# Attention's products with V in plain fp32, two heads on two column halves, in a fused attention, Fourier and MLP kernel

## The chip, the core and the metric

The kernel runs on one core of a Trainium2 chip. The core has TensorE (PE in the rows, its weight loads as PEld), VectorE (DVE), ScalarE (ACT), GpSimd (POOL) and SyncE (SP, which issues DMAs here). The metric is the device time of one execution in microseconds, as the median of several runs. One further execution was taken by the profiler, and all rows come from it.

## The reference

Three blocks in a row: attention that keeps only scores close to the row's maximum, a Fourier mixing with an MLP, and a token mixing. The change lies in the first.

```python
def _attn_ref(q, k, v, tau):           # q, k, v: 4 x 8 heads x 576 x 64
    scores = 1.0 / np.sqrt(64) * np.matmul(q, k.transpose(0, 1, 3, 2))
    thresh = np.max(scores, axis=-1, keepdims=True) - tau
    scores = np.where(scores >= thresh, scores, -1000000000.0)
    attn = np.exp(scores - np.max(scores, axis=-1, keepdims=True))
    attn = attn / (np.sum(attn, axis=-1, keepdims=True) + 1e-09)
    return np.matmul(attn, v)

def _moe_ref(x, w_ch1, w_ch2):
    u = x + np.real(np.fft.fft(np.fft.fft(x, axis=1), axis=2))
    un = (u - mean(u)) / np.sqrt(var(u) + 1e-06)
    return u + np.maximum(un @ w_ch1, 0.0) @ w_ch2

def _moe2_ref(x, w_theta, w_tok_r, w_tok_i, w_ch):
    theta = x @ w_theta
    u = x + w_tok_r @ (x * cos(theta)) + w_tok_i @ (x * sin(theta))
    return u + np.maximum(u @ w_ch, 0.0)
```

## The kernel before

The 32 heads are taken as 16 pairs. A pair has nine score tiles of 128 queries by 576 keys. For each tile, TensorE makes the scores (lines 457 and 458: a high and a low part of the keys, in the type fp32r), VectorE takes the row maximum (467), ScalarE the exponential (472), VectorE the mask and the row sum (481), TensorE transposes the tile P in four blocks of 128 keys (488), and ScalarE copies the transposed block out of PSUM (499). The last 64 keys of each head are transposed apart (`rest_ops`, line 546) into `pt5`.

The products with V work on split numbers. `hi` writes the high part of the transposed P, rounded to fp32r, and `lo` subtracts it to get the low part (508; on VectorE, or for two tiles of nine on GpSimd from an extra copy `plain`, 503). V is split in the same way by ScalarE (416) and GpSimd (419), and high and low parts lie side by side as 128 weight columns. A pair has four products `pv`: for each head a half of 256 queries and a half of 320. Three of them (592, 595) multiply the 128 columns of V with the high and with the low part of P. The fourth, of head 0 and the first half (`WHOLE`), multiplies P as one fp32 number (583) for the four whole key blocks, and takes parts for the rest (587). A product comes out of PSUM in two pieces: ScalarE copies one 64-row part (601), VectorE adds the other (605). GpSimd multiplies the finished pair with the reciprocal row sums R (676) into `xT`.

When four pairs are done, a batch is done, and its Fourier transform (lines 723 to 946, tiles X, Y, u) runs among the work of later pairs; the last batch's runs after the last pair. Then come the MLP (h at line 1187, acc at 1207 to 1209) and the token mixing. The MLP's weights are widened on ScalarE, VectorE and GpSimd (1056 to 1090), from the end of the attention on.

The order on every engine is made before the program is written: `Plan.schedule` takes the operations with estimated costs, due times (`pr`) and a table of corrections `SHIFT`, lets an engine wait up to `PATIENCE` for an operation that is due earlier, and writes each engine's instructions in the order found. On the chip every engine keeps that order. Score tiles use two PSUM buffers, transposes and products share four banks (tag `O`).

Of the kernel before, what the change touches and what calls it, by code (L numbers as in the profile page):

```python
# [97 lines left out]
class Plan:  # L98
# [160 lines left out]
    PATIENCE = {"PE": 20, "DVE": 0, "ACT": 80, "POOL": 520, "SP": 460}  # L259


def attention_and_fft(pl, tc, ident, tb, pss, left, middle, right, qk, vv, cfk, cst, csr, u_d):
# [22 lines left out]
    Q, V, VR, xTs = {}, {}, {}, {}  # L285
# [120 lines left out]
    def load_v(p):  # L406
        loc = {}
        prio = [pr(9 * p - 9 + d if p else -8 + i, s) for i, (d, s) in enumerate(LOADS[7:])]

        def dma(e):  # L410
            VR[p] = loc["vr"] = new("vr", [128, 12, 64], f"vr{p}")
            e.dma_start(loc["vr"][:], vv[p])

        def hi(e):
            V[p] = new("v", [128, 12, 2, 64], f"v{p}", F32R)
            e.copy(V[p][:, :, 0], loc["vr"][:])

        def lo(e):
            e.tensor_sub(V[p][:, :, 1], loc["vr"][:], f32(V[p][:, :, 0]))

        pl.op(("vr", p), "SP", 1000, prio[0], dma, new=[("vr", p)], delay=8000)
        pl.op(("hv", p), "ACT", act(768, False), prio[1], hi, [("vr", p)], [("v", p)], [("vr", p)])
        pl.op(("lv", p), "POOL", pool(768), prio[2], lo, [("hv", p)], (), [("vr", p), ("v", p)])


    def pair(p):
        g0 = 9 * p
        st = {}

        def ptiles(h, half):  # L430
            return [(f"p{t}{h}{half}", p) for t in ("h" if (h, half) in WHOLE[p] else "hl")]

        def tile_ops(idx):
# [10 lines left out]
            parted = [d for d in dests if d[:2] not in WHOLE[p]]  # L444
# [46 lines left out]
            def hi(e):  # L491
                for h, half in fresh:
                    for t, _ in ptiles(h, half):
                        st[t[1], h, half] = new(t, [128, 4, 320 if half else 256], f"{t}_{p}",
                                                F32 if (h, half) in WHOLE[p] else F32R)
                    if not half:
                        st["r", h] = new("pt5", [128, 2, 320], f"pt5{p}_{h}", F32R)
                for h, half, qc, c0, w in dests:
                    e.copy(st["h", h, half][:, :, qc:qc + w], loc["T"][:, :, c0:c0 + w])

            def plain(e):
                tf = new("tf", [128, 4, 128], f"tf{p}_{idx}")
                e.copy(tf[:], loc["T"])
                loc["T"] = tf

            def lo(e):
# [7 lines left out]
            made = [x for f in fresh for x in ptiles(*f)] + [("pt5", p, h) for h, half in fresh if not half]  # L514
            hs = [x for d in dests for x in ptiles(*d[:2])]
# [10 lines left out]
            after, lo_on, src = "turn", "DVE", T  # L526
            if idx in YSET[p] and parted:
                src, after, lo_on = ("tf", k), "plain", "POOL"
                pl.op(("plain", k), "ACT", act(512), pr(g + 2, 5), plain, [("turn", k)], [src], [T])
            pl.op(("hi", k), "ACT", act(512, after == "turn") + 40 * (len(dests) - 1), pr(g + 2, 5), hi,  # L530
                  [(after, k)] + [("hi", (p, i)) for i in his], made, [src] + [x for x in hs if x not in made])
            if parted:
                w = 4 * sum(d[4] for d in parted)
                pl.op(("lo", k), lo_on, (dve if lo_on == "DVE" else pool)(w) + 40 * (len(parted) - 1), pr(g + 2, 8), lo,
                      [("hi", k)], (), [src] + hs)

        def rest_ops(h, idxs, g):
# [11 lines left out]
            def parts():  # L549
                if tail:  # L550
                    return [(st["r", i], slice(256, 320), loc["T"][:, 64 * i:64 * i + 64]) for i in range(2)]
                return [(st["r", h], slice(0, 256), loc["T"][:, 0:256])]

            def hi(e):
                for pt5, c, src in parts():
                    e.copy(pt5[:, 0, c], src)

            def lo(e):
                for pt5, c, src in parts():
                    e.tensor_sub(pt5[:, 1, c], src, f32(pt5[:, 0, c]))  # L560
# [7 lines left out]
            pl.op(("hi", k), "ACT", act(64) * 2 if tail else act(256), pr(g, 5), hi, [("turn", k)] + before, (), [T] + hs)  # L568
            pl.op(("lo", k), "DVE", dve(64) * 2 if tail else dve(256), pr(g, 8), lo, [("hi", k)], (), [T] + hs)

        def pv_ops(h, half, g):
# [26 lines left out]
            def copy(e):  # L598
                if (h, half) == (0, 0):
                    st["t"] = new("t", [128, S], f"t{p}")  # L600
# [1240 lines left out]
```

## Time and profile before

| what | value |
|---|---|
| median of 3 runs | 1022.69 us (1021.73 to 1023.72) |
| the profiled execution: time | 1019.57 us |
| its span, first to last instruction | 1017.7 us |
| mean granted clock of TensorE | 0.994 |
| TensorE busy | 979.6 us, 96% |
| VectorE busy | 702.4 us, 69% |
| ScalarE busy | 500.0 us, 49% |
| GpSimd busy | 293.9 us, 29% |

The profile page gives busy times over the whole span, then the costliest groups of instructions by line. A group names what is written and read (`O<-ph,v`), the shape, the count, the busy time and the mean of one instruction, and the idle time just ahead of it. Queries of the trace give busy times in chosen windows, instructions in order of time, and the chain of work that ended last. Durations of neighbours overlap, since engines are pipelined: what an instruction costs in a row of its like is the distance to the next start. The ends of matmuls are modelled.

### The profile page before, as it was taken

How to read it: one execution, taken by the hardware profiler on the slowest of the kernel's cores; microseconds unless marked ns; L12 is line 12 of the kernel's file. 1: busy time of each engine (PE TensorE's matmuls, PEld its weight loads, DVE VectorE, ACT ScalarE, POOL GpSimd, SP SyncE). 2: the span in 40 equal slices, each digit the busy share in tenths (PEclk: the TensorE clock that was granted, in tenths of full speed). 3: DMA queues.
4: the chain of work that ended last, by engine and by line, in shares of the span. 5: the costliest groups of instructions: out<-in, count | busy, mean ns of one | idle time of the engine just before them, and what ended most of it. 6: DMA issues, size and time to landing. Idle time of an engine off the chain costs nothing.

```text
span 1017.7 us, 16444 instructions
## 1 busy us (share of the span) xinstructions
PE 979.6 (96%) x5952; PEld 882.8 (87%) x5952; DVE 702.4 (69%) x1418; ACT 500.0 (49%) x961; POOL 293.9 (29%) x435
## 2 busy tenths in 40 slices
PE   5998899999999979999999999999999999999998
PEld 4888899999999868888888888899988999999998
DVE  6999999999999999997564452311245567766732
ACT  6898988889887744433231131111133333353410
POOL 5676867745864541012000000000000011121100
PEclk9999999999999989999999999999999999999999
DMA  7796555564652455454751353200305402011011
GB/s 204 211 226 150 151 132 149 148 182 116 159 130 58 129 185 174 166 185 167 244 201 61 102 193 113 73 1 1 119 19 209 164 22 61 29 43 56 17 41 48
DMA packets 49984, 123.15 MB, mean 121 GB/s; under 512 B 7088, under 2 KB 11760, under 8 KB 49520
## 3 DMA queue, kind: packets, MB, share of 16 engines
q1 hardware_dynamic: 49184, 119.08, 39.3%
q0 software_dynamic: 720, 3.02, 1.1%
q8 instruction: 47, 0.77, 0.3%
q14 instruction: 33, 0.27, 0.1%
HBM read 69.84 MB, written 23.66 MB: 92 GB/s over the span
## 4 chain that ended last, share of the span: by engine, by line
PE 74%; DVE 13%; ACT 6%; issue 2%; DMA 2%; POOL 1%; SPq 1%; ACTq 0%; DVEq 0%; POOLq 0%
PE h L1187 20%; PE y L1462 11%; PE acc L1209 7%; PE acc L1208 7%; PE acc L1207 7%; PE f L1526 5%; PE th L1338 5%; DVE c L467 4%; DVE P L481 4%; ACT P L472 2%; PE T L488 2%; PE ps L457 2%; PE ps L458 1%; PE O L592 1%; DVE pl L508 1%
## 5 line engine op out<-in xcount | busy, mean ns | idle before, releaser
L1187 PE MATMUL h<-uh,w 128*128 128x512 f32 (+1 forms) x640 | 199.1, 372 | 0.0
L1196 DVE SCALAR_TENSOR_TENSOR hl<-h,hh 128x512 fp32r<-128x512 f32 (+1 forms) x80 | 50.9, 637 | 156.5 <-ACT hh L1192 156.4
L1192 ACT ACTIVATE hh<-h 128x512 fp32r<-128x512 f32 (+1 forms) x80 | 44.4, 555 | 224.4 <-PE h L1187 224.4
L1187 PEld LDWEIGHTS h<-uh,w 128*128 128x128 f32 x640 | 118.9, 188 | 17.0
L457 PE MATMUL ps<-H,L 128*128 128x288 f32 x320 | 100.7, 332 | 20.5 <-DVE P L481 9.8
L1187 PE MATMUL h<-ul,w 128*128 128x512 f32 (+1 forms) x320 | 118.4, 370 | 0.0
L481 DVE SCALAR_TENSOR_TENSOR P<-ps,c,P 128x576 f32<-128x576 f32 x144 | 114.3, 809 | 5.1 <-ACT P L472 2.7
L472 ACT ACTIVATE P<-ps,c 128x576 f32<-128x576 f32 x144 | 106.3, 749 | 15.5 <-DVE c L467 14.7
L1207 PE MATMUL acc<-w,hh 128*128 128x512 f32 x288 | 113.6, 395 | 0.0
L1209 PE MATMUL acc<-w,hl 128*128 128x512 f32 x288 | 113.3, 393 | 0.0
L1208 PE MATMUL acc<-w,hh 128*128 128x512 f32 x288 | 113.2, 393 | 0.0
L467 DVE TENSOR_REDUCE c<-ps 128x1 f32<-128x576 f32 x144 | 106.5, 751 | 5.7 <-PE ps L458 4.6
L1462 PE MATMUL y<-w,z 128*128 128x288 f32 x768 | 109.8, 296 | 0.0
L1462 PEld LDWEIGHTS y<-w,z 128*128 128x128 f32 x768 | 104.5, 188 | 0.8
L458 PE MATMUL ps<-X,L 128*128 128x288 f32 x320 | 90.5, 300 | 0.3 <-DVE X L393 0.3
L488 PE MATMUL T<-ident,P 128*128 128x128 f32 x576 | 86.0, 278 | 2.2 <-DVE P L481 1.1
L457 PEld LDWEIGHTS ps<-H,L 128*128 128x128 f32 x320 | 61.9, 193 | 27.8 <-ACT H L390 7.2
L1370 POOL TENSOR_TENSOR tok<-tok 128x512 f32<-128x512 f32 x8 | 10.3, 1293 | 231.8 <-DVE tok L1342 122.2
L488 PEld LDWEIGHTS T<-ident,P 128*128 128x128 f32 x576 | 68.6, 142 | 6.6 <-DVE P L481 1.4
L1139 POOL TENSOR_SCALAR mv<-mv 128x1 f32<-128x1 f32 x18 | 9.3, 519 | 206.9 <-DVE mv L1135 206.6
L1187 PEld LDWEIGHTS h<-ul,w 128*128 128x128 f32 x320 | 60.2, 188 | 9.0
L1209 PEld LDWEIGHTS acc<-w,hl 128*128 128x128 f32 x288 | 54.0, 188 | 12.5 <-DVE hl L1196 0.2
(384 smaller groups left out, 2144.3 us busy)
## 6 DMA issues: line engine op xcount, KB each, us to landing
H<-hs SPq DMA_DIRECT2D x60, 160.0 KB
X<-raw SPq DMA_DIRECT2D x60, 160.0 KB
raw<-in_qk SPq DMA_DIRECT2D x15, 608.0 KB
vr<-in_vv SPq DMA_DIRECT2D x16, 384.0 KB
w<-w_d SPq DMA_DIRECT2D x6, 992.0 KB
mu<-u_d SPq DMA_DIRECT2D x18, 256.0 KB
ru<-u_d SPq DMA_DIRECT2D x18, 256.0 KB
x_d<-ru SPq DMA_DIRECT2D x18, 256.0 KB
```

Source lines behind the costliest of these rows:

```text
L457: e.matmul(ps[:, half, :HS], L[:, qo:qo + 128], H[:, ko:ko + HS], start=(j == 0), stop=False)
L458: e.matmul(ps[:, half, :HS], L[:, qo:qo + 128], X[:, ko:ko + HS], start=False, stop=(j == n - 1))
L467: e.tensor_reduce(loc["c4"][:, 0:1], loc["ps"][:, :, :HS], axis=AXES.XY, op=ALU.max, negate=True)
L472: e.activation(halves(), loc["ps"][:, :, :HS], AF.Exp, bias=loc["c4"][:, 0:1], scale=1.0)
L481: e.scalar_tensor_tensor(halves(), loc["ps"][:, :, :HS], loc["c4"][:, 1:2], halves(), op0=ALU.is_ge, op1=ALU.mult, accum_out=st["sums"][:, ...
L488: e.transpose(T[:, kt * 128:(kt + 1) * 128], P[:, kt * 128:(kt + 1) * 128], ident[:])
L1187: e.matmul(loc["ps"][:, :n], a, x[:, c, :n], start=(k == 0), stop=(k == 11))
L1196: e.scalar_tensor_tensor(loc["hl"][:, :n], loc["ps"][:, :n], 0.0, f32(loc["hh"][:, :n]), op0=ALU.max, op1=ALU.subtract)
L1207: e.matmul(a, hh[:, q], wh, start=(f == 0), stop=False)
L1208: e.matmul(a, hh[:, q], wl, start=False, stop=False)
L1209: e.matmul(a, hl[:, q], wh, start=False, stop=(f == NF - 1))
L1462: e.matmul(loc["ps"][:, half, :HS], z[:, cs], w, start=(n == 0 and m == 0), stop=(n == 8 and m == 2))
```

## The change

V and the transposed P are no longer split. One copy per tile writes the transposed P in plain fp32, and `plain`, both `lo` operations, the split of V, and the buffers for low parts are gone. The buffers for the transposed P are doubled. A pair has two products instead of four: one for the 256 queries of the first half and one for the 320 of the second, each over both heads. In each, five key blocks are multiplied in plain fp32 with 64 columns of V; head 0 writes partitions 0 to 63 of the bank and head 1 partitions 64 to 127, in turn. The result is multiplied with R by VectorE straight out of PSUM into `xT`; the copies, additions and the multiplication on GpSimd are gone. `PATIENCE` changes, and `SHIFT` gets further rows.

```diff
-    PATIENCE = {"PE": 20, "DVE": 0, "ACT": 80, "POOL": 520, "SP": 460}
+    PATIENCE = {"PE": 40, "DVE": 0, "ACT": 300, "POOL": 300, "SP": 210}
...
-    for t, n in dict(raw=2, hs=2, L=2, H=2, X=2, vr=2, v=2, P=3, pt5=2, t=1, R=1, tf=1,
+    for t, n in dict(raw=2, hs=2, L=2, H=2, X=2, vr=2, P=3, pt5=4, R=1,
...
-        for t in "h" if all((h, half) in WHOLE[p] for p in range(NP)) else "hl":
-            pl.tag(f"p{t}{h}{half}", 1)
+        pl.tag(f"p{h}{half}", 2)
...
-        pl.op(("hv", p), "ACT", act(768, False), prio[1], hi, [("vr", p)], [("v", p)], [("vr", p)])
-        pl.op(("lv", p), "POOL", pool(768), prio[2], lo, [("hv", p)], (), [("vr", p), ("v", p)])
...
-            def lo(e):
-                for h, half, qc, c0, w in parted:
-                    e.tensor_sub(st["l", h, half][:, :, qc:qc + w], loc["T"][:, :, c0:c0 + w],
-                                 f32(st["h", h, half][:, :, qc:qc + w]))
...
-        def pv_ops(h, half, g):
+        def pv_ops(half, g):
...
-                if whole:
-                    for kt in range(4):
-                        e.matmul(O[:, :n], VR[p][:, h * 6 + kt:h * 6 + kt + 2].rearrange("p a b->p (a b)"), st["h", h, half][:, kt],
-                                 start=(kt == 0), stop=False)
...
-                else:
-                    for kt in range(4):
-                        vk = v[:, h * 6 + kt].rearrange("p a b->p (a b)")
-                        for t in "hl":
-                            e.matmul(O[:, :n], vk, st[t, h, half][:, kt], start=(kt == 0 and t == "h"), stop=False)
...
+                O = loc["O"] = pl.bank([128, 512], f"O{p}_{half}")
+                for kt in range(5):
+                    for h in range(2):
+                        w, x = VR[p][:, h * 6 + (kt if kt < 4 else 4 + half)], st[h, half][:, kt] if kt < 4 else st["r", h][:, :n]
+                        e.matmul(O[64 * h:64 * h + 64, :n], w, x, start=(kt == 0), stop=(kt == 4))
+
+            def mul(e):
+                if (j, half) == (0, 0):
+                    xTs[b] = new("xT", [128, 4, S], f"xT{b}")
+                e.tensor_mul(xTs[b][:, j, a:a + n], loc["O"][:, :n], st["R"][:, a:a + n])
...
+            idxs = ((0, 2, 5, 7), (1, 3, 4, 6, 8))[half]
+            deps = [("hi", (p, i)) for i in idxs] + [("hi", (p, "r", i)) for i in ((0, 1), (0, 1, 2))[half]]
+            pl.op(("pv", k), "PE", 5 * TWO_PASS * n / 256 + 250, pr(g, 3), mms, deps + [("vr", p)], [O],
...
-        for h, gs in ((0, (g0 + 7, g0 + 8)), (1, (g0 + 11, g0 + 13))):
-            for half in range(2):
-                pv_ops(h, half, gs[half])
-        scale_op(g0 + 14)
+        for half in range(2):
+            pv_ops(half, g0 + 12 + 1.5 * half)
```

The names in the rows below: `ps` are scores, `P` masked tiles, `T` transposes, `O` products, `ph`, `pl` and `pt` (before) or `pt` alone (after) the transposed P, `pt5` its last key block, `v` the split V, `vr` V as loaded, `R` the reciprocal sums, `c` maxima. The number behind a name is the pair.

TensorE at the end of the last pair, before: the first two products follow the last scores.

```order
L458 MATMUL ps15_6_5296<-X15_4729,L15_4689 128x288
L583 MATMUL O15_0_0_5319<-ph00_15_5133,vr15_4605 128x256 x4
L587 MATMUL O15_0_0_5319<-pt515_0_5134,v15_4898 128x256 x3
L592 MATMUL O15_0_1_5333<-ph01_15_5135,v15_4898 128x320
L592 MATMUL O15_0_1_5333<-pl01_15_5136,v15_4898 128x320
L592 MATMUL O15_0_1_5333<-ph01_15_5135,v15_4898 128x320
L592 MATMUL O15_0_1_5333<-pl01_15_5136,v15_4898 128x320
L592 MATMUL O15_0_1_5333<-ph01_15_5135,v15_4898 128x320
L592 MATMUL O15_0_1_5333<-pl01_15_5136,v15_4898 128x320
L592 MATMUL O15_0_1_5333<-ph01_15_5135,v15_4898 128x320
L592 MATMUL O15_0_1_5333<-pl01_15_5136,v15_4898 128x320
L595 MATMUL O15_0_1_5333<-pt515_0_5134,v15_4898 128x320 x2
```

The same place after, behind all transposes of the pair:

```order
L580 MATMUL R15_0_4640<-ident_66,R15_4619 128x128 x4
L540 MATMUL O15_0_4650<-pt15_00_4385,vr15_4248 64x256
L540 MATMUL O15_0_4650<-pt15_10_4423,vr15_4248 64x256
L540 MATMUL O15_0_4650<-pt15_00_4385,vr15_4248 64x256
L540 MATMUL O15_0_4650<-pt15_10_4423,vr15_4248 64x256
L540 MATMUL O15_0_4650<-pt15_00_4385,vr15_4248 64x256
L540 MATMUL O15_0_4650<-pt15_10_4423,vr15_4248 64x256
L540 MATMUL O15_0_4650<-pt15_00_4385,vr15_4248 64x256
L540 MATMUL O15_0_4650<-pt15_10_4423,vr15_4248 64x256
L540 MATMUL O15_0_4650<-pt515_0_4386,vr15_4248 64x256
L540 MATMUL O15_0_4650<-pt515_1_4424,vr15_4248 64x256
L582 MATMUL R15_1_4670<-ident_66,rr15_4601 128x128
```

The products moved behind the transposes of the whole pair, and the heads stand in turn.

VectorE among the first tiles of pair 8, before, with the additions (605) and low parts (508, 560) of pairs 7 and 8:

```order
L605 TENSOR_TENSOR t7_2551<-O7_1_0_2669,t7_2551 64x256
L467 TENSOR_REDUCE c48_3_2732<-ps8_3_2719 128x1
L508 TENSOR_TENSOR pl11_7_2524<-T7_8_2652,ph11_7_2523 128x4x128
L467 TENSOR_REDUCE c48_4_2755<-ps8_4_2736 128x1
L869 TENSOR_TENSOR u0_0_1_2772<-xt0_0_1_2727,sm0_0_2657 128x256
L871 TENSOR_TENSOR u0_0_1_2772<-xt0_0_1_2727,dm0_0_2255 128x4x63
L873 TENSOR_TENSOR u0_0_1_2772<-xt0_0_1_2727,dm0_0_2255 128x4
L481 SCALAR_TENSOR_TENSOR P8_2_2681,sums8_2575<-ps8_3_2719,c48_3_2732,P8_2_2681 128x576
L481 SCALAR_TENSOR_TENSOR P8_4_2777,sums8_2575<-ps8_4_2736,c48_4_2755,P8_4_2777 128x576
L605 TENSOR_TENSOR t7_2551<-O7_1_1_2759,t7_2551 64x320
L560 TENSOR_TENSOR pt58_0_2713<-T58_0_2804,pt58_0_2713 128x256
L467 TENSOR_REDUCE c48_5_2832<-ps8_5_2814 128x1
```

The same place after:

```order
L451 TENSOR_REDUCE c48_1_2383<-ps8_1_2367 128x1
L460 TENSOR_SCALAR c48_1_2383<-c48_1_2383,tb_71 128x1
L451 TENSOR_REDUCE c48_4_2398<-ps8_4_2374 128x1
L465 SCALAR_TENSOR_TENSOR P8_0_2265,sums8_2229<-ps8_1_2367,c48_1_2383,P8_0_2265 128x576
L465 SCALAR_TENSOR_TENSOR P8_4_2402,sums8_2229<-ps8_4_2374,c48_4_2398,P8_4_2402 128x576
L545 TENSOR_TENSOR xT1_1514<-O7_0_2387,R7_2319 128x256
L545 TENSOR_TENSOR xT1_1514<-O7_1_2346,R7_2319 128x320
L451 TENSOR_REDUCE c48_5_2423<-ps8_5_2411 128x1
```

Between maxima and masks only the two multiplications of pair 7 are left, behind the masks of pair 8's first five tiles.

## Rows read from the trace of the kernel before

**Rows 1.** The page's part 1: busy us (share of the span) xinstructions

```profile
PE 979.6 (96%) x5952; PEld 882.8 (87%) x5952; DVE 702.4 (69%) x1418; ACT 500.0 (49%) x961; POOL 293.9 (29%) x435
```

**Rows 2.** Busy us by window; at the end clock, DMA share, GB/s

```profile
core 0: us, PE busy (x) PEld busy (x) DVE busy (x) ACT busy (x) POOL busy (x), PEclk, DMA share, GB/s
...
45.00:100.00 55.00, 49.52 (x349) 44.99 (x348) 51.54 (x120) 49.60 (x104) 41.07 (x65) 1.00 0.78 195
100.00:200.00 100.00, 95.14 (x707) 89.44 (x706) 96.33 (x229) 88.86 (x187) 72.59 (x114) 1.00 0.54 141
200.00:300.00 100.00, 97.88 (x738) 93.23 (x738) 96.18 (x232) 86.80 (x182) 67.63 (x105) 1.00 0.59 152
...
345.00:390.00 45.00, 38.21 (x247) 33.21 (x246) 42.32 (x84) 21.02 (x39) 18.72 (x20) 0.92 0.61 198
390.00:1018.00 628.00, 623.46 (x3406) 552.28 (x3404) 337.31 (x576) 184.97 (x316) 45.75 (x48) 1.00 0.30 99
```

**Rows 3.** Line L583, plain fp32 products: ns min/median/max, first and last start

```profile
L583 PE MATMUL O<-ph,vr x128: 377/379/484, 24.1 to 343.6; 128*128 128x256 f32 x128
```

**Rows 4.** Chain of waits, 40 to 130 us: start us, us, what

```profile
55.83 7.79 DMA X<-raw
...
122.11 1.73 PE O L583 x8
```

**Rows 5.** TensorE in order of time, last pair: start us, us, what

```profile
341.98 1.99 PE L583 MATMUL O<-ph,vr 128*128 128x256 f32 x8 [0.21 <-DVE pt L560]
...
344.17 0.31 PE L592 MATMUL O<-ph,v 128*128 128x320 f32 x1
...
345.63 1.03 PE L488 MATMUL T<-ident,P 128*128 128x128 f32 x8
...
350.47 0.28 PE L592 MATMUL O<-ph,v 128*128 128x256 f32 x1
...
351.66 0.31 PE L592 MATMUL O<-ph,v 128*128 128x320 f32 x1
...
353.13 0.40 PE L849 MATMUL Yt<-xho,cts 128*128 128x258 f32 x2
```

**Rows 6.** TensorE in order of time, 336.2 to 336.6 us

```profile
336.28 0.28 PE L821 MATMUL Xo<-ctr,eys 128*31 128x258 f32 x1
336.40 0.28 PE L821 MATMUL Xo<-ctr,exs 128*31 128x258 f32 x1
336.53 0.27 PE L546 MATMUL T<-ident,P 128*128 128x128 f32 x1
```

**Rows 7.** Groups of instructions: busy us, mean ns | idle before us

```profile
L508 DVE TENSOR_TENSOR pl<-T,ph 128x512 fp32r<-128x512 f32 (+1 forms) x96 | 55.4, 594 | 0.3
...
L508 POOL TENSOR_TENSOR pl<-tf,ph 128x512 fp32r<-128x512 f32 x32 | 41.2, 1288 | 11.2 <-ACT ph L499 7.3 <-PE T L488 2.4 <-issue 1.3
...
L419 POOL TENSOR_TENSOR v<-vr,v 128x768 fp32r<-128x768 f32 x16 | 29.5, 1844 | 8.7 <-ACT v L416 8.7
L601 ACT COPY t<-O 64x256 f32<-64x256 f32 x64 | 25.2, 394 | 9.7 <-PE O L595 6.7 <-PE O L587 1.2 <-POOL xT L676 0.6
L676 POOL TENSOR_TENSOR xT<-t,R 128x576 f32<-128x576 f32 x16 | 23.9, 1492 | 5.6 <-DVE t L605 3.4 <-ACT R L656 2.2
...
L605 DVE TENSOR_TENSOR t<-O,t 64x320 f32<-64x320 f32 (+1 forms) x48 | 22.4, 467 | 2.0 <-ACT t L601 0.8
...
L560 DVE TENSOR_TENSOR pt<-T,pt 128x256 fp32r<-128x256 f32 (+1 forms) x64 | 18.9, 316 | 2.1 <-ACT pt L556 1.7
...
L503 ACT COPY tf<-T 128x512 f32<-128x512 f32 x32 | 18.9, 589 | 1.4 <-PE T L488 1.1
...
L416 ACT CAST v<-vr 128x768 fp32r<-128x768 f32 x16 | 13.4, 837 | 0.2
```

**Rows 8.** In order of time after the last product

```profile
355.05 2.46 POOL L676 TENSOR_TENSOR xT<-t,R 128x576 f32<-128x576 f32 x1 [3.35 <-DVE t L605]
...
358.41 0.42 DVE L723 TENSOR_TENSOR go<-xT 128x256 f32<-128x256 f32 x1
```

More of the change, by code (lines that the diff above doesn't have):

```diff
@@ L513, in tile_ops @@
             ps, P, T = ("ps", k), ("P", (p, couple)), ("O", "T", k)
-            made = [x for f in fresh for x in ptiles(*f)] + [("pt5", p, h) for h, half in fresh if not half]
-            hs = [x for d in dests for x in ptiles(*d[:2])]
+            made = [(f"p{h}{half}", p) for h, half in fresh] + [("pt5", p, h) for h, half in fresh if not half]
+            hs = [(f"p{h}{half}", p) for h, half, *_ in dests]
             his = sorted({(0, 4)[d[0]] for d in dests} - {idx})
@@ L525, in tile_ops @@
             pl.op(("turn", k), "PE", 428, pr(g + 2, 1), turn, [("mask", k)], [T], [P])
[L526 to L535, printed above, removed]
+            pl.op(("hi", k), "ACT", act(512) + 40 * (len(dests) - 1), pr(g + 2, 5), copy,
+                  [("turn", k)] + [("hi", (p, i)) for i in his], made, [T] + [x for x in hs if x not in made])
         def rest_ops(h, idxs, g):
@@ L547, in turn, with copy @@
                 loc["T"] = T
-            def parts():
+            def copy(e):
+                T = loc["T"]
                 if tail:
[L551 to L560, printed above, removed]
+                    for i in range(2):
+                        e.copy(st["r", i][:, 256:320], T[:, 64 * i:64 * i + 64])
+                else:
+                    e.copy(st["r", h][:, 0:256], T[:, 0:256])
             T = ("O", "T", p, "r", h)
@@ L596, in mms @@
-                loc["O"] = O
-            def copy(e):
-                if (h, half) == (0, 0):
-                    st["t"] = new("t", [128, S], f"t{p}")
-                e.copy(st["t"][r0:r0 + 64, a:a + n], loc["O"][rows, :n])
-            def add(e):
-                th = st["t"][r0:r0 + 64, a:a + n]
-                e.tensor_add(th, loc["O"][r0:r0 + 64, :n], th)
-            k = (p, h, half)
-            O, t = ("O", k), ("t", p)
-            idxs = ((0, 2), (1, 3, 4), (5, 7), (6, 8, 4))[2 * h + half]
@@ L610, in pv_ops @@
-            whole = (h, half) in WHOLE[p]
-            rows = slice(0, 64) if whole else slice(r1, r1 + 64)
-            deps = [("hi" if whole else "lo", (p, i)) for i in idxs] + [("lo", (p, "r", h))] + ([("lo", (p, "r", 2))] if half else [])
-            first = (h, half) == (0, 0)
-            pl.op(("pv", k), "PE", 4 * TWO_PASS * n / 256 + mm(3, n) + 150 if whole else mm(10, n), pr(g, 3), mms, deps + [("lv", p)], [O],
-                  [("v", p), ("pt5", p, h)] + ptiles(h, half) + ([("vr", p)] if whole else []))
@@ L616, in pv_ops @@
-            pl.op(("ocopy", k), "ACT", act(n), pr(g + 1, 4.2), copy,
-                  [("pv", k)] + ([] if first else [("ocopy", (p, 0, 0))]), [t] if first else [], [O] if first else [O, t])
-            if not whole:
-                pl.op(("oadd", k), "DVE", dve(n) + 70, pr(g + 1, 7.5), add, [("ocopy", k)], (), [O, t])
+                O = loc["O"] = pl.bank([128, 512], f"O{p}_{half}")
[3 more added lines that the diff above has]
+                        e.matmul(O[64 * h:64 * h + 64, :n], w, x, start=(kt == 0), stop=(kt == 4))
@@ L621, in norm_ops @@
+            after = [("pv", k), ("Rc", p, half)] + ([("mu", p)] if half else []) + ([("mul", 4 * b)] if j else [])
+            made = [xT] if (j, half) == (0, 0) else []
+            pl.op(("mul" if half else "mu", p), "DVE", dve(n), pr(g + 1, 7.5), mul, after, made,
+                  [O, ("R", p)] + ([] if made else [xT]))
         def norm_ops(g):
```

72 lines of the change are left out of this document (20 added, 52 removed), and 14 rows, old and new, of the table SHIFT.

## The prediction

> **What bounds the kernel now.** I start with the page's busy shares: TensorE (PE) is busy 96% of the span, VectorE (DVE) 69%, ScalarE (ACT) 49%, GpSimd (POOL) 29% [rows 1]. These are averages over stages, so the next view is the table by windows [rows 2]. From 390 us on, outside the reach of this change, TensorE is busy nearly all the time and VectorE far less. In the attention stage the picture is another one: between 100 and 300 us TensorE is busy 95.14 + 97.88 = 193.0 of 200 us and VectorE 96.33 + 96.18 = 192.5; ScalarE has 175.7 and GpSimd 140.2. Two engines share the bound there, and taking work off one alone would buy little. The change takes much off VectorE, ScalarE and GpSimd and alters TensorE's products, so the forecast hangs on what TensorE gains or loses.
>
> The pace of a pair comes from the plain fp32 products, one group per pair: the first starts at 24.1 us [rows 3], that of pair 5 at about 122.1 [rows 4], that of pair 15 at 342.0 [rows 5]. That is 98.0/5 = 19.6 us a pair while TensorE does attention alone, and 219.9/10 = 22.0 us once the transform of the finished batches is mixed in. So the 200 us window holds some 9.1 pairs: 21.2 us of TensorE and 21.2 of VectorE for each pair, in 22.0 us. In the early pairs the window from 45 to 100 us gives 49.52/55 of 19.6 = 17.6 us of TensorE and 51.54/55 = 18.4 us of VectorE a pair, with the DMA engines at a share of 0.78 against 0.54 and 0.59 later [rows 2]. The chain of waits has a 7.79 us load of X there [rows 4].
>
> **Part by part. TensorE, removed.** The four products of the last pair, by the distance from their first matmul to what follows: 341.98 to 344.17, to 345.63, then 350.47 to 351.66, to 353.13 [rows 5]. That is 2.19 + 1.46 + 1.19 + 1.47 = 6.31 us a pair.
>
> **TensorE, added.** Each pair now has two products, for 256 and 320 columns, of five row blocks and two heads: 10 plain fp32 matmuls each. The trace shows that a plain fp32 matmul runs as two instructions (x128 for 16 pairs of four, [rows 3]), and eight of them at 256 columns take 1.73 us [rows 4], 0.216 each; at 320 columns I scale to 0.270. No row shows two matmuls side by side on two column halves, so the price has two ends. One after the other: 20 x 0.216 + 20 x 0.270 = 9.72 us a pair. Overlapped: the halves alternate in the order printed above, the second instruction of one head runs beside the first of the other, and 20 instructions take 11 slots: 11 x (0.216 + 0.270) = 5.35 us. Nothing goes below 10 slots, 4.86 us. A narrow weight alone saves no time: the transform's matmuls with 31 weight columns start 0.12 and 0.13 us apart [rows 6], the pace of 258 columns streamed. So the gain has to come from overlap. I take 5.35: the two halves hold weights of their own, write partitions of their own, and no operand is handed from one to the other. This is a choice and not a reading; both ends stay in the range. By it TensorE gains 6.31 - 5.35 = 0.96 us a pair; by the other end it loses 3.41.
>
> **VectorE, ScalarE, GpSimd.** From the groups of instructions [rows 7], each sum divided by 16 pairs. VectorE loses the low parts and the additions, 55.4 + 18.9 + 22.4 = 96.7 us or 6.04 a pair, and gets two multiplications out of PSUM per pair, which I price like the additions there, 2 x 0.467 = 0.93: from 21.2 to 16.1 us a pair. ScalarE loses the extra copies, the copies of the products and the high part of V, 18.9 + 25.2 + 13.4 = 57.5 us or 3.6 a pair; its copies of P stay. GpSimd loses 41.2 + 29.5 + 23.9 = 94.6 us or 5.9 a pair. The load of V stays. The copies of P without their low parts cost nothing new: TensorE's 20 us cover them. The buffers for the transposed P are doubled, so a product that waits for all nine tiles of its pair lets the next pair's tiles be copied meanwhile.
>
> **What is late next.** With 16.1 us VectorE stands well under TensorE's 21.2 - 0.96 = 20.2. Before, each of the two filled 96% of the pace. With TensorE alone at the bound I let it fill 97.5%: 20.2/0.975 = 20.75, 1.25 us less than 22.0, and over ten pairs -12.5 us. Early: (17.6 - 0.96)/0.95 = 17.5 would be -2.1 us a pair, but the loads are heaviest there, and if they set the pace nothing is won; about half, -1.1 over five pairs, -5.5 us. At the end, the way from the last product's end (353.13) over the addition, the multiplication on GpSimd (2.46 us) to the first VectorE fold at 358.41 is 5.3 us [rows 5, 8]; one multiplication on VectorE with its waits takes about 1.0 instead, -4.3. Against it, both products (5.35 us) now stand behind the last transposes, where only two of four (1.19 + 1.47 = 2.66) stood, +2.7. VectorE, busy 42.32 of the 45 us from 345 to 390 [rows 2], is rid of some 2 us of low parts and additions there: -2.0. Together -3.6. **The sum** is -12.5 - 5.5 - 3.6 = -21.6 us. Against the profiled execution's 1019.57 us (span 1017.7) that is 998.0; the median of the runs stands 3.1 us above it (1022.69), so 1001.
>
> **Waits moved.** Each product now waits for the copies of both heads, and behind it on TensorE stand the next pair's scores. The order puts the product among the next pair's scores and transposes, two to four tiles on, so its operands are old when it comes up; it is the last pair that has nothing to hide behind, and that is in the sum. The multiplication on VectorE stands behind the masks of the next pair's first tiles and holds one of four banks that long; since VectorE has 4 us a pair to spare, I cost that at nothing, and at 0.4 us a pair (one multiplication late) if the cover fails.
>
> **Rivals.** (1) Serial halves, the other side. If the array runs the two heads one after the other, a pair costs TensorE 21.2 + 3.41 = 24.6 us, at 97.5% a pace of 25.2: +3.2 x 10 = +32. Early (17.6 + 3.41)/0.95 = 22.1, +2.5 x 5 = +12.5; the end +7.1 - 4.3 - 2.0 = +0.8. Together +45: 1068 us. The change is paid off up to about 6.8 us of products a pair: there ten pairs lose about what the early pairs and the end win. For it: every matmul of the trace follows the one before at the full streaming time, none shows overlap. Against it: weight loads are busy 87% and matmuls 96% of the span [rows 1], so the loads run beside matmuls and the array does hold two things at once.
>
> (2) Overlap with losses at each change of shape. A product enters the 64-column shape and leaves it, four changes a pair. If each waits until the matmul before has left the array, the price is a matmul's duration less its pace, about 0.28 - 0.12 = 0.16 us [rows 6], 0.64 a pair: products 6.0 us, TensorE 20.9, pace 21.4, -0.6 x 10 = -6; early half of -1.4 x 5 = -3.5; end -3.0. Together -12.5: 1010 us. Against it: the change from 31 to 128 columns at 336.40 to 336.53 us shows no such wait [rows 6]. [...]
>
> (3) The loads keep the first five pairs at 19.6 us: the -5.5 falls away, 1007 us. For it: the load of X in the chain of waits and the DMA share of 0.78 [rows 2, 4]. Against it: that share is not 1, and the same bytes would need 0.87 at 17.5 us a pair.
>
> **How the numbers follow.** Forecast 0.60; losses at shape changes 0.13; loads 0.08; serial 0.17; nothing measurable 0.02. The first three make 0.81, of which I give 0.02 to a form too weak to see and 0.01 to one that turns over: faster 0.78, same 0.04, slower 0.18 (0.2%, 2 us, is about what a measurement of this kernel can tell). The forecast's own spread downward: the early pairs at the full -2.1 give 5 us more, TensorE filling 99% instead of 97.5% 3 us more, and if the modelled ends of matmuls (0.16 us past the next start, at the end of every group) overstate TensorE's work by 5%, 1 us a pair, 16 us more: 976 or 977. Upward it takes in the rivals at 1007 and 1010 and goes toward the serial end as far as a product price of about 7.2 us, 1030. The serial end itself, 0.17, is left out.
>
> **What would show it.** In the profile after: the distance from the first matmul of a product to what follows, 2.4 and 3.0 us if overlapped, 4.3 and 5.4 if serial; the starts of the two halves' instructions nearly together or 0.216 apart. The pace of a pair at 20 to 21 us late and 17.5 to 19.6 early. VectorE at some 75 to 80% from 100 to 300 us, TensorE still at 96% or more. The stage from 390 us on shifted as a whole and as long as before; if it changes its length, a cause that I don't have is at work. The prediction is wrong if the products take over 6.8 us a pair, or if TensorE shows idle time before scores that wait for copies or masks.

## The result and the profile after

| | before | after |
|---|---|---|
| median | 1022.21 us (1018.77 to 1023.72) | 1007.72 us (1006.33 to 1009.77) |
| ratio | 1 | 0.9865 (95%: 0.9834 to 0.9895) |
| profiled execution, span | 1019.57, 1017.7 us | 1009.77, 1007.7 us |

The change makes the kernel 14.5 us faster by the medians, 10.0 us by the two spans. The forecast was 21.6 us. The profiled execution of the changed kernel was the slowest of its four (1009.77 us), and that of the kernel before stood under its median; the stretches below come from these two and so add up to 10.0 us, not to 14.5.

To see where the time went I cut each span at three instants: the first score (L457 before, L441 after) of pair 0, of pair 5 and of pair 15. The instants are from the records of the single instructions, rounded to 0.1 us.

| us | to pair 0 | pairs 0 to 4 | pairs 5 to 14 | pair 15 to the end |
|---|---|---|---|---|
| before | 7.2 | 103.7 | 213.8 | 693.0 |
| after | 7.1 | 109.3 | 198.3 | 693.0 |
| difference | -0.1 | **+5.6** | **-15.5** | 0.0 |

The ten late pairs won more than forecast (-12.5), the five early pairs lost where a gain was forecast (-5.5), and the end won nothing (-3.6 forecast). Page, part 1, of the changed kernel, answering [rows 1]:

```profile
PE 960.8 (95%) x5936; PEld 830.0 (82%) x5936; DVE 641.0 (64%) x1276; ACT 446.0 (44%) x842; POOL 206.0 (20%) x344
```

The table by windows, answering [rows 2] (busy us and instructions of each engine, then clock, DMA share, GB/s):

```profile
core 0: us, PE busy (x) PEld busy (x) DVE busy (x) ACT busy (x) POOL busy (x), PEclk, DMA share, GB/s
45.00:100.00 55.00, 38.87 (x276) 31.07 (x277) 35.17 (x84) 35.25 (x72) 22.92 (x41) 0.91 0.73 171
100.00:200.00 100.00, 97.82 (x772) 80.44 (x770) 83.21 (x195) 77.15 (x160) 50.46 (x95) 1.00 0.61 157
200.00:300.00 100.00, 98.22 (x772) 82.54 (x772) 84.62 (x200) 74.82 (x157) 44.38 (x89) 1.00 0.63 159
345.00:390.00 45.00, 37.63 (x238) 32.06 (x238) 44.16 (x86) 19.86 (x31) 16.36 (x14) 1.00 0.57 181
390.00:1008.00 618.00, 613.66 (x3353) 544.22 (x3351) 327.10 (x559) 181.31 (x311) 39.93 (x44) 1.00 0.29 98
```

From 100 to 300 us TensorE is now the only full engine (98%), and VectorE fell from 96% to 84%, where 75 to 80% was forecast. From 45 to 100 us TensorE fell from 49.52 to 38.87 us: something stands still there. First the products, in TensorE's order of time; the groups at 101.24 and 109.35 are the two products of one pair:

```profile
100.27 1.03 PE L472 MATMUL T<-ident,P 128*128 128x128 f32 x8
101.24 2.38 PE L540 MATMUL O<-pt,vr 128*64 128x256 f32 x20
103.55 0.40 PE L441 MATMUL ps<-H,L 128*128 128x288 f32 x1
...
109.35 2.91 PE L540 MATMUL O<-pt,vr 128*64 128x320 f32 x20
112.19 0.65 PE L472 MATMUL T<-ident,P 128*128 128x128 f32 x4
```

From start to next start the two groups take 2.31 and 2.84 us, 5.15 together. That is the overlapped end of the forecast's price. In the single records the instructions start in twos, 6 to 7 ns apart (by their order of issue presumably one of each column half; the records don't name the half), and every two take 0.216 us (256 columns) or 0.269 (320). Then the early gap, on TensorE, VectorE, ScalarE and SyncE:

```profile
64.74 0.29 PE L442 MATMUL ps<-X,L 128*128 128x288 f32 x1
75.06 1.11 PE L472 MATMUL T<-ident,P 128*128 128x128 f32 x4 [10.03 <-DVE P L465]
...
74.17 0.82 DVE L465 SCALAR_TENSOR_TENSOR P<-ps,c,P 128x576 f32<-128x576 f32 x1 [8.35 <-ACT P L456]
...
72.74 0.77 ACT L303 ACTIVATE raw<-raw,tb 128x576 f32<-128x576 f32 x1 [8.75 <-issue]
73.42 0.72 ACT L456 ACTIVATE P<-ps,c 128x576 f32<-128x576 f32 x1
...
57.07 0.46 SPq L340 DMA_DIRECT2D X<-raw  x1
68.32 0.33 SPq L298 DMA_DIRECT2D raw<-in_qk  x1
68.70 0.43 SPq L408 DMA_DIRECT2D vr<-in_vv  x1
```

Read backwards: TensorE waits 10.03 us for a mask, the mask 8.35 us for an exponential (L456), and the exponential stands on ScalarE behind L303, the scaling of pair 5's raw tile. "Issue" at L303 is the wait for a load: the raw load went out only at 68.32, when the last placing of pair 3's X (issued 57.07) had landed and set the buffer free. Nothing in pair 2 needs pair 5's tile; its exponentials for tiles 7 and 8 merely stand behind it in one queue. In the kernel before, ScalarE does the last two exponentials of pair 2 first, and then the scaling (there L304) waits 0.48 us for its load:

```profile
65.92 1.41 ACT L472 ACTIVATE P<-ps,c 128x576 f32<-128x576 f32 x2 [0.42 <-DVE c L467]
67.81 0.78 ACT L304 ACTIVATE raw<-raw,tb 128x576 f32<-128x576 f32 x1 [0.48 <-DMA raw<-in_qk]
```

So the rows show ScalarE working in the order of its queue: in the changed kernel the scores are done by 65.03 us (64.74 + 0.29) and the last maximum by 65.82, and the two exponentials that read them start at 73.42 and 74.51, behind the scaling and its wait of 8.75 us.

### The profile page after: what moved, and what is told of

Same layout as the page of the kernel before. It is cut to its first block, busy times and chain, and to the rows that moved or that the text cites. A ratio compares the mean times of both kernels' runs of the same rounds, so it can differ in the third digit from the quotient of the medians.

```text
span 1007.7 us, 15996 instructions
## 1 busy us (share of the span) xinstructions
PE 960.8 (95%) x5936; PEld 830.0 (82%) x5936; DVE 641.0 (64%) x1276; ACT 446.0 (44%) x842; POOL 206.0 (20%) x344
## 4 chain that ended last, share of the span: by engine, by line
PE 63%; DVE 0%; DVEq 0%; issue 0%
PE h L1105 20%; PE y L1380 11%; PE acc L1127 7%; PE acc L1126 7%; PE acc L1125 7%; PE f L1444 5%; PE th L1256 5%; PE xT L1231 1%; PE uT L1067 1%; DVE ul L1078 0%; PE Ye L770 0%; PE Yo L770 0%; PE xt L783 0%; DVE v('w', 3)_4928 L978 0%; DVE bs L1052 0%; PE xt_t L783 0%
## 5 line engine op out<-in xcount | busy, mean ns | idle before, releaser
L1105 PE MATMUL h<-uh,w 128*128 128x512 f32 (+1 forms) x640 | 198.6, 372 | 0.0
L1110 ACT ACTIVATE hh<-h 128x512 fp32r<-128x512 f32 (+1 forms) x80 | 44.3, 555 | 224.3 <-PE h L1105 198.3
L456 ACT ACTIVATE P<-ps,c 128x576 f32<-128x576 f32 x144 | 106.1, 744 | 29.5 <-DVE c L451 26.9
L441 PE MATMUL ps<-H,L 128*128 128x288 f32 x320 | 101.8, 335 | 15.8 <-DVE P L465 8.4
L481 ACT COPY pt<-T 128x512 f32<-128x512 f32 (+1 forms) x160 | 83.0, 550 | 21.5 <-PE T L472 20.8
L472 PEld LDWEIGHTS T<-ident,P 128*128 128x128 f32 x576 | 69.2, 144 | 19.9 <-DVE P L465 14.9
L540 PE MATMUL O<-pt,vr 128*64 128x256 f32 (+1 forms) x640 | 85.3, 413 | 0.0
L441 PEld LDWEIGHTS ps<-H,L 128*128 128x128 f32 x320 | 62.7, 196 | 22.1 <-issue 9.7
L540 PEld LDWEIGHTS O<-pt,vr 128*64 128x64 f32 x640 | 43.4, 138 | 31.1 <-issue 4.8
```

The costliest lines, as they stand in the source:

```text
L441: e.matmul(ps[:, half, :HS], L[:, qo:qo + 128], H[:, ko:ko + HS], start=(j == 0), stop=False)
L456: e.activation(halves(), loc["ps"][:, :, :HS], AF.Exp, bias=loc["c4"][:, 0:1], scale=1.0)
L472: e.transpose(T[:, kt * 128:(kt + 1) * 128], P[:, kt * 128:(kt + 1) * 128], ident[:])
L540: e.matmul(O[64 * h:64 * h + 64, :n], w, x, start=(kt == 0), stop=(kt == 4))
L1105: e.matmul(loc["ps"][:, :n], a, x[:, c, :n], start=(k == 0), stop=(k == 11))
```

## Experiments

Each stretch below is cut as in the second table; the ratio is to the kernel before, measured beside each; stretches are of one profiled execution each.

| kernel | median us | ratio (95%) | 0 to 4 | 5 to 14 | 15 to end |
|---|---|---|---|---|---|
| changed | 1007.72 | 0.9865 (0.9834 to 0.9895) | 109.3 | 198.3 | 693.0 |
| e1 scaling later | 1002.45 | 0.9825 (0.9807 to 0.9844) | 100.0 | 198.6 | 693.9 |
| e2 values earlier | 1006.67 | 0.9861 (0.9844 to 0.9878) | 108.1 | 198.3 | 692.5 |
| e3 both | 1000.46 | 0.9816 (0.9793 to 0.9839) | 99.7 | 197.6 | 692.4 |
| e4 tables later | 1002.87 | 0.9825 (0.9808 to 0.9842) | 101.2 | 198.6 | 692.7 |
| e9 all three | 999.84 | 0.9790 (0.9774 to 0.9806) | 99.6 | 198.2 | 692.7 |
| e5 halves in series | 1048.41 | 1.0258 (1.0235 to 1.0282) | 114.0 | 227.1 | 697.6 |
| e6 before, no low parts | 1013.83 | 0.9923 (0.9902 to 0.9944) | 101.6 | 208.8 | 692.7 |
| e7 VectorE loaded | 1065.73 | 1.0418 (1.0392 to 1.0443) | 119.6 | 241.0 | 696.5 |
| e11 loaded less | 1046.50 | 1.0250 (1.0228 to 1.0272) | 115.3 | 228.5 | 693.8 |
| e8 old waiting times | 1023.39 | 1.0018 (1.0002 to 1.0034) | 106.5 | 210.3 | 697.7 |
| e12 ScalarE's alone | 1027.48 | 1.0062 (1.0048 to 1.0075) | 107.6 | 205.1 | 705.1 |
| e10 before, new times | 1055.06 | 1.0322 (1.0302 to 1.0342) | 116.4 | 221.4 | 708.8 |

### The early gap: e1 to e4, e9

The plan stays; single operations are moved in the finished order of emission.

```diff
         ops, order = self.ops, self.schedule()
+        self.move(order, ('kq', 5), 0, ('hq', 5))           # e1, e3, e9
+        self.move(order, ('vr', 2), 1, ('raw', 4))          # e2, e3, e9
+        self.move(order, ('table', 3), 1, ('raw', 7))       # e4, e9
+        self.move(order, ('table', 4), 1, ('table', 3))     # e4, e9
```

> The changed kernel with one instruction in another place: ScalarE's scaling of pair 5's raw tile (L303) stands directly ahead of its rounding (L309) instead of ahead of the exponentials of pair 2's tiles 7 and 8. Theory: ScalarE's 8.75 us wait for the raw load held these two exponentials, their masks and TensorE, so the 10.0 us gap on TensorE ahead of 75.06 us closes; pair 3's first score comes at 66 to 69 us instead of 75.8. Pair 2's values, issued on SyncE behind the same raw load (68.7 us), then hold TensorE for up to 5 us, so that of the 10 us 4 to 6 stay: median 1002 to 1004 us against 1007.7. Rival, loads set the pace here: the gap only moves to pair 4's first score, which stays at 94 to 96 us, and the time stays at 1006 to 1009.

> The changed kernel with only the load of pair 2's values (L408) moved on SyncE, from behind pair 5's raw load to behind pair 4's (42 us). Theory: nothing waits for these values as long as ScalarE stands still until 72.7 us, so the gap of 10.0 us on TensorE stays, and the time is that of the changed kernel, 1006 to 1009 us. Rival, the values of pair 2 were what the kernel waited for: the gap shrinks by 5 us or more, 1000 to 1003.

> Both moves together: pair 5's scaling behind the exponentials, pair 2's values loaded early. Theory: the gap ahead of 75 us goes with nothing in its place, pair 3's first score at 66 to 68 us, pair 4's at 86 to 90 us (96.1 in the changed kernel), and 7 to 9 us of the time go: 999 to 1001 us, which is the gain of the first five pairs that the prediction had. Rival, loads set the pace: pair 4's L, H and X, issued behind the raw load, come no sooner, pair 4's first score stays at 94 to 96 us, and the time at 1006 to 1009.

> The changed kernel with two of the five table loads (cts, second half, 768 KB, and ctr, 384 KB; L914) issued on GpSimd some 50 us later, everything else in place. Theory: pair 3's last X load took 11.2 us to land because the first and second half of cts were issued 3.6 us apart just before it (9.2 us apart in the kernel before, where it took 7.8 us); without the second half it lands 3 to 4 us sooner, pair 5's raw load is issued at 64 to 66 us instead of 68.3, the gap on TensorE shrinks by as much, and the time is 1004 to 1005 us. Rival, the placing loads of pair 3 fill the queues by themselves: the raw load stays at 67 to 69 us and the time at 1006 to 1009.

> The changed kernel with all three moves: pair 5's scaling behind the exponentials of pair 2, pair 2's values loaded early, the second half of cts and ctr loaded some 50 us later. Theory, with the first two moves the first five pairs already run at 19.9 us each, which is the late pace that TensorE sets, so the third has nothing left to take: 998 to 1002 us, pair 5's first score at 106 to 107 us. Rival, the moves add up (5.3 + 4.9 us): 995 to 997.5.

TensorE, ScalarE and SyncE of e3 (L309 is its scaling, L304 its raw load), then of e4, both around the place of the old gap:

```profile
67.78 0.66 PE L478 MATMUL T<-ident,P 128*128 128x128 f32 x4 [1.58 <-DVE P L471]
71.61 0.77 ACT L309 ACTIVATE raw<-raw,tb 128x576 f32<-128x576 f32 x1
65.72 0.33 SPq L304 DMA_DIRECT2D raw<-in_qk  x1
```

```profile
69.33 0.66 PE L478 MATMUL T<-ident,P 128*128 128x128 f32 x4 [3.37 <-DVE P L471]
67.02 0.78 ACT L309 ACTIVATE raw<-raw,tb 128x576 f32<-128x576 f32 x1 [2.10 <-issue]
58.73 0.46 SPq L346 DMA_DIRECT2D X<-raw  x1
62.94 0.33 SPq L304 DMA_DIRECT2D raw<-in_qk  x1
```

With the scaling behind the exponentials (e1) the gap of 10.03 us is gone, and what is left of it is a wait of 1.61 us ahead of pair 2's first product at 70.41. I had expected pair 2's values to keep 4 to 6 us of it, so that half of the theory failed, though the time fell inside its range. In e3 that one goes too, and pair 3's first score stands at 68.2 us instead of 75.8, pair 4's at 86.3 instead of 96.1: loads do not set the pace there. The values alone (e2) change the median by 0.1%, inside the intervals, though in its profiled execution the gap was split (5.59 us there, 2.81 earlier). e4 reaches the same gap from the other side. It leaves the queues as they are but issues two table loads later: the last X of pair 3 lands 4.2 us after its issue (58.73 to 62.94) instead of 11.2, the scaling waits 2.10 us instead of 8.75, and TensorE's gap shrinks to 3.37 us, by more than the 3 to 4 us expected. In e9, with the tables late too, the same X takes 4.9 us, in e1, e2 and e3, with the tables in place, 7.3 to 10.5. So the chain runs table loads, X, raw load, ScalarE, exponentials, and it can be cut at either end. e9 holds all three moves and gains nothing measurable over e3; its early pairs run at 19.9 us, as in e3, which is the late pace. e9 is faster than both kernels: its interval lies clear of the changed kernel's, while those of e1, e3 and e4 still touch it. By the ratios the moves are worth 0.4 to 0.75% (4 to 8 us), less than the 8 to 10 us that the early stretches show, in part because the changed kernel's profiled execution was the slowest of its four.

### Is the gain overlap? e5

```diff
-                for kt in range(5):
-                    for h in range(2):
+                for h in range(2):
+                    for kt in range(5):
```

> The changed kernel with the loop of the products (L540) turned inside out: the five key blocks of head 0, then the five of head 1, so that neighbours no longer use different column halves. Same instructions, same count, same columns. Theory, the two halves run at the same time: alone a product takes 0.216 us for 256 columns and 0.270 for 320, so 20 of them take 4.3 and 5.4 us against 2.31 and 2.84, 4.5 us more for each pair; TensorE sets the pace, the late pairs go from 19.8 to 24.2 to 24.5 us, and the time is 1070 to 1082 us. Rival, the halves do not overlap and the gain is that of fewer, narrower products: a group takes the same 2.3 and 2.8 us, and the time is that of the changed kernel, 1005 to 1010.

TensorE of e5, the two groups of a pair:

```profile
123.52 4.58 PE L540 MATMUL O<-pt,vr 128*64 128x320 f32 x20
128.03 0.32 PE L582 MATMUL R<-ident,rr 128*128 128x128 f32 x1
...
129.79 3.73 PE L540 MATMUL O<-pt,vr 128*64 128x256 f32 x20
133.44 0.40 PE L441 MATMUL ps<-H,L 128*128 128x288 f32 x1
```

The same instructions in another order take 4.51 and 3.65 us, 8.16 against 5.15, and the kernel is slower than the one before. The rival without overlap is out. My number was too high (1070 to 1082 us, 9.7 us of products a pair; the late pace is 22.7 us, not 24.2 to 24.5), and the single records say why: most instructions follow each other by 0.216 us, but around the change of heads eight of the twenty start as four twos. Four slots are saved, where strict order would let only the last instruction of head 0 and the first of head 1 meet. The records don't tell the heads apart. If each of the four twos holds one instruction of each head, since those of one head follow each other by 0.216 us elsewhere, TensorE doesn't keep the written order there to the instruction, as I had said of every engine.

### VectorE's share: e6, e7, e11

e6 takes the low parts off VectorE and GpSimd but leaves TensorE's work; e7 and e11 leave the changed products but give VectorE work back.

```diff
             def lo(e):                                       # e6, both places
-                e.tensor_sub(...)
+                pass
...
             def mask(e):                                     # e7; e11 with 352 columns
                 ...
+                part = st["P", couple][:, c0:c0 + 512]
+                e.tensor_sub(junk[:], part, part)
```

> The kernel before without the instructions that make the low parts of P (L508 and L560, VectorE and GpSimd); the products read the high part in their place, so TensorE's instructions and the plan are unchanged, and the output leaves out the low parts of P. VectorE is relieved of 4.8 us a pair. Theory, TensorE sets the pace of the late pairs: it idles only 0.54 us of each 21.4 us there, so the pace falls by at most that, to 20.9 to 21.3 us, and the time to 1012 to 1020 us. Rival, VectorE's work was the bound and its relief is the whole gain: the pace falls to under 20.5 us and the time to 1003 to 1010.

> The changed kernel with VectorE's dropped work put back: behind every mask (L465) one subtraction of 128x512 elements whose result nobody reads, nine a pair, some 5.3 us a pair, so that VectorE has 21.5 to 22 us of work for a pair against 19.6 on TensorE. Theory, both halves of the change are needed: VectorE becomes the bound, the late pace goes back from 19.8 to 21.5 to 22.5 us, VectorE is over 95% busy from 100 to 300 us, and the time is 1020 to 1035 us. Rival, VectorE's relief is worth nothing and TensorE's shorter products are all: the pace stays at 19.8 to 20.3 us and the time at 1007 to 1012.

> As the kernel with VectorE's dropped work put back, but with subtractions of 128x352 instead of 128x512 elements: those took 0.79 us each, 7.1 us a pair, more than the 5.4 that the change took off VectorE; these should take 0.55 to 0.60, 5.0 to 5.4 a pair. Theory, VectorE at its old load binds: it was 95% busy at a pace of 24.1 us, 22.9 us of work; with 2.0 less the pace is 21.5 to 22.3 and the time 1025 to 1042 us, slower than the kernel before, so that TensorE's shorter products alone give nothing. Rival, the excess alone made it slow: the pace is 19.8 to 20.6 and the time 1007 to 1015.

Windows of e6, then of e11, then e11's added subtraction among VectorE's groups from 100 to 300 us (mean ns behind the busy us):

```profile
100.00:200.00 100.00, 96.14 (x724) 91.58 (x723) 81.21 (x183) 90.76 (x193) 62.22 (x108) 1.00 0.56 145
200.00:300.00 100.00, 98.77 (x754) 95.09 (x753) 82.25 (x192) 87.46 (x184) 54.09 (x97) 1.00 0.58 151
```

```profile
100.00:200.00 100.00, 88.55 (x657) 69.07 (x656) 94.52 (x211) 68.31 (x141) 45.91 (x80) 1.00 0.55 137
200.00:300.00 100.00, 90.95 (x675) 71.91 (x675) 94.99 (x210) 64.09 (x132) 44.31 (x78) 0.98 0.56 146
...
L469 DVE TENSOR_TENSOR junk<-P 128x352 f32<-128x352 f32 x79 | 50.4, 637 | 2.7
```

Relief alone (e6) takes the late pace from 21.4 to 20.9 us and is worth 0.8%; TensorE is at 96 to 99% there and stops it; VectorE now waits 17.2 us for scores between 110 and 320 us, where it waited 1.1. In e11 VectorE is full at 95%, TensorE idles, and the pace is 22.8 us. But both runs gave VectorE more than the change had taken. e7's subtractions took 790 ns, 7.1 us a pair instead of the 5.4 that I wanted (the 594 ns by which I had priced them is a mean over two shapes), e11's 637 ns, 5.7 a pair. By busy time, in which neighbours that overlap count once, VectorE has 20.6 us a pair before, 16.7 after, 21.7 in e11 and 23.2 in e7; so the change took 3.9 off, and e11 stands 1.2 above the old load. From e7 to e11 1.4 us less work on VectorE gave a pace 1.25 us shorter, so VectorE sets it in both. Carried on in that proportion to 20.6 us, an estimate, the pace would be 21.8 against 21.4 before: by it the shorter products alone gain nothing with VectorE at its old load. The added subtractions are not in the plan, which may cost something of its own; that part was not separated.

### The waiting times: e8, e10, e12

The diff also changes the planner's PATIENCE, by which an engine's next operation may be held for a more urgent one. My sum had no term for it.

```diff
-    PATIENCE = {"PE": 40, "DVE": 0, "ACT": 300, "POOL": 300, "SP": 210}
+    PATIENCE = {"PE": 20, "DVE": 0, "ACT": 80, "POOL": 520, "SP": 460}    # e8; e10 the reverse, in the kernel before
+    PATIENCE = {"PE": 40, "DVE": 0, "ACT": 80, "POOL": 300, "SP": 210}    # e12
```

> The changed kernel planned with the waiting times (PATIENCE) of the kernel before. Pair 5's scaling still stands on ScalarE ahead of the exponentials of pair 2's tiles 7 and 8 in this order. Theory, the gap comes from a load that lands later than the planner believes, not from the planner's new waiting times: a gap of 8 to 12 us on TensorE near 65 to 76 us stays, and the time is within 0.5% of the changed kernel, 1003 to 1013 us. Rival, the new waiting times made the gap: it is gone, and the time is 998 to 1001 us.

> The kernel before planned with the waiting times (PATIENCE) of the changed kernel, all else as before. With the old waiting times the changed kernel ran no faster than the kernel before (1.002), so the question is what the new ones are worth alone. Theory, they fit only the changed set of operations: the kernel before gains nothing by them, 1019 us or more (1019 to 1050). Rival, the new waiting times are better by themselves and carry the gain: 1005 to 1013 us.

> The changed kernel with one of the four waiting times put back: ScalarE's 80 instead of 300, the other three as changed. With all four put back VectorE waited for an exponential 19 times, 7.0 us, between 110 and 320 us, against 7 times, 2.3 us, with the new ones, and the late pace was 21.0 us. Theory, ScalarE's waiting time carries the loss: with 80 the plan lets copies and roundings that are ready go ahead of an exponential that is about to be, the late pace is 20.7 us or more and the time 1015 to 1030 us. Rival, the loss is from GpSimd's and SyncE's waiting times, which order the loads and the small bounds: the late pace stays at 19.8 to 20.2 us and the time at 1003 to 1011.

With the old waiting times the changed kernel is no faster than the kernel before (e8). The theory held for the gap (scaling still ahead, TensorE's wait 6.79 us) and failed for the time: the late pace is 21.0 instead of 19.8 us, and the end 4.7 us longer. The kernel before with the new times is 3.2% slower (e10; 1055 us, past the 1050 that I had set), so they aren't better by themselves; they go with the changed plan. The diff also adds some 80 rows to SHIFT, for nearly every kind of operation, and doubles buffers. e8 and e12 keep these, so they don't say what the old waiting times would give with rows chosen for them, and neither the rows nor the buffers were tested apart. VectorE's waits for exponentials between 110 and 320 us, of the changed kernel, of e8 and of e12 (us in all, times, longest):

```profile
DVE P L465 <- ACT P L456: 2.3, 7, 0.7
```

```profile
DVE P L465 <- ACT P L456: 7.0, 19, 0.7
```

```profile
DVE P L465 <- ACT P L456: 6.8, 19, 0.6
```

ScalarE's 80 alone brings these waits back (e12) and more than the whole loss in time, 1027 us; the rival, GpSimd's and SyncE's times, is out as the only cause. But my mechanism covers only part of it: the late pace came out at 20.5 us, under the 20.7 that I had set, and 12.1 us of e12's loss lie behind pair 15's first score, where the order of the last transforms is another one and the granted clock from 345 to 390 us is 0.89 instead of 1.00. What in that order costs them I haven't traced.

## Why the prediction was right and wrong, step by step

**The choice of overlap was right.** 5.15 us a pair measured, 5.35 forecast; e5 shows that the order of the heads makes it. The count behind it was off in two ways that cancel, which is luck. Neighbours overlap in ten slots, not eleven: 10 x (0.216 + 0.270) = 4.86. And the changes of shape that rival 2 priced at 0.64 us a pair do cost time. From the last transposition into a 64-column group, up to its second slot, the records show 0.469 us, where 0.109 + 0.216 = 0.325 would be the plain pace: +0.14. Out of it, the last instruction takes 0.309 instead of 0.216 and the transposition behind it 0.165 instead of 0.109: +0.15. That is 0.29 a group, 0.58 a pair, of which 0.29 stand in the 5.15 and the rest beside it. Between transpositions and scores, both 128 columns wide, the sum is 0.246 against 0.242, and in the kernel before, from transpositions into plain fp32 products of 128 columns, 0.327 against 0.325, so it is the change of shape. So rival 2, at 0.13, had the place of the loss and nearly its price (0.64 us, 0.58 measured), and only the fuller overlap hid it; whether the wait is for the matmul before to leave the array, as it supposed, was not shown. [rows 6], which I held against it, show matmuls of 31 weight columns 0.12 and 0.13 us apart, without a wait, where the records of the 64-column groups show 0.14 and 0.15 us, and so were no evidence on it. Twenty instructions of the two halves in turn took 2.31 us, where 20 x 0.216 = 4.32 would be one after the other: 4.32/2.31 = 1.87 times as fast.

**The late pace was right in kind and too small in size.** Forecast 22.0 to 20.75, measured 21.4 to 19.8, so -1.55 instead of -1.25 a pair. The base of 22.0 was mis-sized: I took the pace from first products, and that of pair 15, with no pair behind it, stood 17.2 us after its first score where pair 5's stood 11.0. In the single records of these ten pairs the products went from 6.46 to 5.15 us (-1.31, where the last pair's 6.31 had given -0.96), and TensorE's idle time from 0.54 to 0.24 (-0.30); the other lines changed by +0.06 together. VectorE's relief was over-sized, 5.1 us a pair by adding up records that overlap, 3.9 by busy time; that did no harm, since TensorE stayed the bound. e6 and e11 say that no such sum of two shares is fair: relief alone gives a third of it, the products alone, by the estimate from e7 and e11, nothing, because both engines were full.

**The early term failed.** -5.5 was forecast for pairs 0 to 4, +5.6 came. The step that failed is "if they set the pace nothing is won": I allowed loads to cancel the gain, not to turn it over, and rival 3 took the loads' share of time as their only cost. What I didn't look at was where operations that wait for a load stand in a queue. In the order before, pair 5's scaling stands behind all exponentials of pair 2 and comes up when its load has all but landed; in the order after, it stands ahead of two of them. The order is fixed before the run and shows this; the trace of before shows the 7.79 us load that made it dangerous [rows 4]. With the place mended (e3, e9) the early pairs give -4.0, near the forecast's -5.5, and the profiled executions come to 998.82 and 999.92 us, where the forecast was 998.0. That the sum comes so close is luck: the late pairs give more than forecast and the end less.

**The end gave 0.0 instead of -3.6.** The step that failed is "about 1.0 instead" for the way from the last product's end to the first fold, -4.3 of the sum. It is 5.3 us before [rows 5, 8] and 4.4 after, -0.9:

```profile
343.85 0.66 PE L783 MATMUL xt<-ident,xT 128*128 128x128 f32 x4
...
344.88 1.23 DVE L982 SCALAR_TENSOR_TENSOR v('w', 0)_4672<-raw('w', 0)_4560,v('w', 0)_4672 128x1024 int32<-128x1024 int32 x1
...
346.75 0.48 DVE L545 TENSOR_TENSOR xT<-O,R 128x320 f32<-128x320 f32 x1
...
348.28 0.42 DVE L644 TENSOR_TENSOR go<-xT 128x256 f32<-128x256 f32 x1
```

The products are done at 343.85, but the multiplication stands on VectorE behind the widening of an MLP weight and starts 2.9 us later. The two other terms lie between the last mask and the last product's end, +0.7 forecast, -0.3 measured (8.5 and 8.2 us). What I had no term for nearly cancels: pair 15 up to its last mask takes 1.0 us more, the way from the fold to the first h 2.9 more (19.8 and 22.7), from the first h to the end it is 2.8 less (639.5 and 636.7). So the stage behind is not quite as long as before, which I had named as the sign of a cause that I don't have; it stays open. In the kernel before, TensorE also spent part of the way to the first h at a lower clock: the granted clock is 0.57 from 366 to 374 us. It was busy 16.93 of the 21 us ahead of that, in the changed kernel 14.45 of them, and there the clock is 1.00 in both windows; what sets it was not shown. The windows of both:

```profile
345.00:366.00 21.00, 16.93 (x129) 14.89 (x127) 20.57 (x47) 10.55 (x21) 11.84 (x17) 1.00 0.69 211
366.00:374.00 8.00, 5.75 (x25) 4.80 (x24) 6.66 (x12) 2.78 (x6) 0.00 (x0) 0.57 0.25 77
```

```profile
345.00:366.00 21.00, 14.45 (x108) 12.48 (x108) 20.73 (x46) 10.47 (x20) 8.66 (x8) 1.00 0.54 170
366.00:374.00 8.00, 7.17 (x48) 6.18 (x48) 7.96 (x16) 2.20 (x5) 3.62 (x3) 1.00 0.74 223
```

**Waits moved** was incomplete: it had nothing on PATIENCE, which by e8 decides 15.7 us, as much as the whole gain, as long as the rows of SHIFT stay as they are.

## What to carry to other kernels

Where two engines are both full, as TensorE at 95 to 98% and VectorE at 96% were here from 100 to 300 us, price a change that takes work off both as one: off VectorE alone it was worth 0.5 us a pair (e6), off TensorE alone nothing, by the estimate above, off both 1.55. After a planner has made a new order, look in it for operations that wait for a load and stand ahead of work that doesn't: one of them cost 9.3 us of the early stretch of the profiled execution here (e1), and moving it and three loads by hand gave a kernel 2.1% faster than before instead of 1.35%. A planner's parameters in a diff are part of the change and need a term, or a bound, of their own.

## What the runs showed of the hardware

- Plain fp32 products of two heads on the two 64-column halves of TensorE run side by side: twenty instructions of 256 columns in 2.31 us, against an estimate of 4.32 (20 x 0.216) one after the other. With one head behind the other (e5) they take 3.65 us, and four slots of twenty are still saved.
- Going into and out of the 64-column shape costs about 0.14 and 0.15 us in the changed kernel, as above.
- Around the end of the early gap TensorE's granted clock is lower. The window, of the changed kernel:

```profile
70.00:81.00 11.00, 5.94 (x28) 5.00 (x30) 4.15 (x10) 5.98 (x11) 1.04 (x3) 0.53 1.01 293
```

TensorE had stood still since about 65 us, and the granted clock from 70 to 81 us is 0.53 (0.50 from 70.3 to 80.5); the scores that start at 75.82 take 0.59 us instead of 0.37 to 0.40. With 5.94 us of work in this window at 0.53 of the clock, an estimate of the price is 5.94 x 0.47 = 2.8 us on top of the 10 us. In e1, e3, e4 and e9, without the gap of 10.03 us, the mean from 45 to 100 us is 1.00, against 0.91 in the changed kernel.
- Without two table loads issued on GpSimd, the last placing load of pair 3, issued on SyncE, landed sooner: the load of raw that waits for the last X of pair 3 went out 11.2 us after that X in the changed kernel, 7.3 to 10.5 in e1 to e3, and 4.2 and 4.9 us after it with the last two tables issued later (e4, e9).
